# An output tile's matmuls set around another block's mixing products, and ten weight subtractions moved from VectorE to GpSimd

## The chip, the cores and the metric

The kernel runs on one core of a Trainium2 chip. The metric is device time in microseconds (us) of one execution, the median over several. The core has five engines with queues of their own, and each works its queue in order: TensorE (PE, with its weight loads shown as PEld), VectorE (DVE), ScalarE (ACT), GpSimd (POOL) and SyncE (SP), which here only issues DMAs. What one engine owes another is told by semaphores.

## What is computed

Three blocks follow each other on two sequences of 768 tokens with 512 features: local attention with a few global columns, then a mixing layer over tokens and channels, then a second mixing layer with a gate. From the reference, cut to what matters here:

```python
# first mixing layer: U 768x32, V 32x768, w_ch1 512x2048, w_ch2 2048x512
xt = x.transpose(0, 2, 1)
h = xt @ U @ V
u = x + h.transpose(0, 2, 1)
ch = np.maximum(u @ w_ch1, 0.0) @ w_ch2
x = u + ch
# second mixing layer: w_k 512x1024, w_v 1024x512, w_r 512x512
xk = mu_k * x + (1.0 - mu_k) * x_prev
xr = mu_r * x + (1.0 - mu_r) * x_prev
k = np.maximum(xk @ w_k, 0.0)
v = k * k @ w_v
r = 1.0 / (1.0 + np.exp(-(xr @ w_r)))
out = r * v
```

The weights come as 64-bit floats. "Second block" in the title of the change is the second sequence of the batch: its products `h` with U and V.

## The kernel before, in words

**Numbers in two parts.** Every float32 factor of a large product is held as a high part (rounded to TensorE's fp32r format) and a low part (the rest), and each product is three matmuls: high by high, high by low, low by high (`PASS`). A weight goes through one conversion (`conv_steps`, lines 645 to 678): a DMA brings a block of 128x512 64-bit floats into a staging tile `stg` (three of them); DVE cuts the lower word (`cvt`, line 655); ACT scales the upper word (`c1`, line 660, tile `cvc`, four of them); DVE joins them (`c2`, line 664) and sets the sign (`c3`, line 668); ACT rounds the high part (line 672); and the low part is a subtraction, high from value (line 676), on POOL or on DVE. A `cvc` tile is free for the fourth conversion after it only when that subtraction has read it.

**Queue of conversions.** `queue_weight` (lines 697 to 709) appends conversions to a list, and `bg` runs them one at a time between other steps. For the weights of the second mixing layer (`wr` 4 blocks, `wk` 8, `wv` 8) every second subtraction is put on DVE by these two lines, the others stay on POOL; those of w1 and w2 are all on POOL:

```python
707  if name in ("wr", "wk", "wv") and kk % 2:
708      steps[-1] = ("lo", lambda z, f=steps[-1][1]: f(z, "DVE"))
```

**The stages.** The attention comes first, planned by a list scheduler of the kernel's own (`Flow`), with the first sequence's mixing products and the first quarter of w1 laid into it. The rest is written out in order by `weave`, which mixes streams of steps; a scheduler of the framework then orders each engine's queue. The token axis of both sequences together is cut into three chunks `c` of 512, the 2048 hidden features into four groups `g`. For each `g`: `ch1` (matmuls into tiles `aps`, line 926; ACT writes the high part of the result `rs`, line 930, DVE the low part, line 934), then `ch2` (`m_ch2`, lines 942 to 952: four output tiles `o`, each 12 matmuls into a PSUM bank `bps`, over four `f` of `rs`, and a DVE addition into the running sum `yp`, line 952). For `g` from 1 on, chunks 1 and 2 of `ch1` go through seven products of sums and differences (tiles `pps`, line 1019, and DVE additions, line 1023).

**PSUM.** There are eight banks of 128x512: four of kind "a" (`aps`, `kps`, `prs`, some `pps`) and four of kind "t" (`bps`, `hps`, `gps`, the other `pps`). A tile waits until the bank that it takes has been read.

**Around the first place of the change.** After the attention, the second sequence is transposed, multiplied by U (`gps`, line 825), and then by V: eight matmuls `hps` (line 856), four of 256 columns and four of 512, each followed by a DVE addition into `yp` (line 861). They are woven with the four output tiles of `ch2` of `g` 0, chunk 0. Three of those tiles come ahead of the 256-column products, the fourth (`o` 3) behind them:

```python
1181  weave(u1[6:8], c0[:1])
1182  weave(c0[1:3])
1183  for kk in range(4):
1184      u1[8 + kk]()                 # hps of 256 columns, kk
1185      u_split(1, kk, slot_d, 1)    # two parts of the sum: ACT line 899, DVE line 901
1186  weave(c0[3:])                    # output tile o 3
1187  weave(u1[12:])                   # the four hps of 512 columns
```

**Around the second place.** The conversions of `wr` and `wk` run during the last quarter (`g` 3) of `ch1` and `ch2`, those of `wv` at the end of `ch2` and during the gate's products (`prs`, line 1241, whose banks ACT frees with the sigmoid, line 1245). After them come `kps` (line 1221) with its low part `kl` on POOL (line 1231), and `pvs` (line 1256). The same code stands a second time in the program for inputs with wider windows; it is not run here.

Of the kernel before, what the change touches and what calls it, by code (L numbers as in the profile page):

```python
# [13 lines left out]
ALU = mybir.AluOpType  # L14
# [195 lines left out]
def body(tc, out, q, k, v, lim, UV, w1, w2, mu_kr, wk, wv, wr):  # L210
    nc = tc.nc
    with ExitStack() as ctx:
# [8 lines left out]
        yp = const.tile([128, 4, 2 * (S + 1)], F32, name="yp")  # L221
# [394 lines left out]
        def path(general):  # L616
            if general:
                attention_general()
            with ExitStack() as pctx, ExitStack() as fence:
# [6 lines left out]
                def bank(tag, nm):  # L626
                    return pp_.tile([128, 512], F32, tag=tag, name=nm, bufs=banks[tag])
# [69 lines left out]
                def queue_weight(name, src, kt, n, sl):  # L697
                    view = [s.rearrange("p (l k n) -> p l k n", l=2, n=n) for s in sl]
                    per = kt // len(sl)
                    wt[name] = (view, per)  # L700
                    for c0 in range(0, n, 512):
                        for kk in range(kt):
                            hi = view[kk // per][:, 0, kk % per, c0:c0 + 512]
                            lo = view[kk // per][:, 1, kk % per, c0:c0 + 512]
                            s = src[kk * 128:(kk + 1) * 128, c0:c0 + 512]
                            steps = conv_steps((128, 512), hi, lo)
                            if name in ("wr", "wk", "wv") and kk % 2:
                                steps[-1] = ("lo", lambda z, f=steps[-1][1]: f(z, "DVE"))
                            bgq.append((lambda d, s=s: nc.sync.dma_start(out=d, in_=s), steps))

                def wsl(name, l, kk, c0, n):
                    view, per = wt[name]
                    return view[kk // per][:, l, kk % per, c0:c0 + n]
# [32 lines left out]
                def queue_g(g, s1, s2):  # L746
                    if s1:
                        queue_weight(("w1", g), w1[:, g * 512:(g + 1) * 512], 4, 512, [s1("w1s")])
                    if s2:
                        queue_weight(("w2", g), w2[g * 512:(g + 1) * 512, :], 4, 512, [s2("w2s")])  # L750
# [156 lines left out]
                def chunk(buf, kk, c, shift=0):  # L907
                    if c == 0:
                        return [(0, 512, buf[:, kk, 1 - shift:513 - shift])]
                    if c == 2:  # L910
                        return [(0, 512, buf[:, kk, 1026 - shift:1538 - shift])]
                    return [(0, 256, buf[:, kk, 513 - shift:769 - shift]),
                            (256, 512, buf[:, kk, 770 - shift:1026 - shift])]


                PASS = ((0, 0), (0, 1), (1, 0))
                NG = 4
                rs = {}
# [13 lines left out]
                def ch1_low(g, c, f):  # L932
                    r = rs[g, c]
                    nc.vector.scalar_tensor_tensor(out=r[:, 1, f, :], in0=rs[g, c, f], scalar=0.0,  # L934
                                                   in1=r[:, 0, f, :].bitcast(F32), op0=ALU.max, op1=ALU.subtract)

                def m_ch1(g, c, f, mk=None):
                    ch1_mm(g, c, f, mk)
                    ch1_high(g, c, f)
                    ch1_low(g, c, f)  # L940

                def m_ch2(g, c, o):
                    r = rs[g, c]
                    ps = bank("t", "bps")
                    n = 0
                    for f in range(4):
                        for lw, lx in PASS:
                            nc.tensor.matmul(ps, lhsT=wsl(("w2", g), lw, f, o * 128, 128), rhs=r[:, lx, f, :],  # L948
                                             start=(n == 0), stop=(n == 11))
                            n += 1  # L950
                    for a, e, ys in chunk(yp, o, c):
                        nc.vector.tensor_tensor(out=ys, in0=ps[:, a:e], in1=ys, op=ALU.add)  # L952

                diffs, sums = [], {}

# [113 lines left out]
                def weave(*streams):  # L1069
                    items = []  # L1070
                    for n, s in enumerate(streams):
                        items += [((x + 0.5) / len(s), n, x, f) for x, f in enumerate(s)]
                    for *_, f in sorted(items, key=lambda v: v[:3]):
                        f()
# [4 lines left out]
                def st_ch2(g, c):  # L1079
                    return [lambda o=o: m_ch2(g, c, o) for o in range(4)]  # L1080
# [96 lines left out]
                u1, c0 = u_steps(1), st_ch2(0, 0)  # L1177
# [2 lines left out]
                    u_split(1, kk, slot_d, 0)  # L1180
                weave(u1[6:8], c0[:1])
                weave(c0[1:3])
                for kk in range(4):
                    u1[8 + kk]()
                    u_split(1, kk, slot_d, 1)
                weave(c0[3:])
                weave(u1[12:])
                actx.close()
                open_slots("sc")
# [117 lines left out]
                assert not bgq  # L1307

        path(False)
        slow = nc.values_load(flag_i[0:1, 0:1], min_val=0, max_val=1)  # L1310
        with tc.If(slow > 0):
            path(True)
# [22 lines left out]
```

## Time and profile before

| | us |
|---|---|
| three runs | 511.73, 511.78, 514.96 |
| median | 511.78 |
| the profiled execution's own time | 512.37 |
| its span, first to last instruction | 510.6 |
| PE busy, matmuls | 495.5 |
| DVE busy | 351.3 |
| ACT busy | 248.4 |
| POOL busy | 166.8 |

The profiled execution took 1.77 us beyond its span, and lies 0.59 us above the median of the runs. The granted TensorE clock is 0.999 over the span. A matmul of 512 columns is recorded at 390 ns, but matmuls overlap: a run of 48 of them in the chain takes 10.88 us, 0.227 us each.

### The profile page before, as it was taken

The numbers are of one execution on the slowest core, as the hardware profiler recorded it, in microseconds if no ns is written. First come the engines' busy times: TensorE is split into PE (matmuls) and PEld (weight loads), VectorE is DVE, ScalarE is ACT, GpSimd is POOL, SyncE is SP. The second block draws the span as 40 slices with busy tenths as digits, with TensorE's granted clock in tenths as the row PEclk, the third lists the DMA queues.
The fourth block names the chain that finished last, engine by engine and source line by source line (L and its number), as shares of the span: only waits on it lengthen the run. The fifth ranks groups of instructions, "written<-read, shape, count | busy, mean of one in ns | idle before, by whom it ended". The sixth has DMA issues, their size and how long they took to land.

```text
span 510.6 us, 8677 instructions
## 1 busy us (share of the span) xinstructions
PE 495.5 (97%) x3278; PEld 403.5 (79%) x3278; DVE 351.3 (69%) x756; ACT 248.4 (49%) x566; POOL 166.8 (33%) x217
## 2 busy tenths in 40 slices
PE   7899999999999999999999999999999999999995
PEld 4677688778877888888888887888888888888885
DVE  7899988999998879558794599999055057301211
ACT  6999986554432533025330275736883167013400
POOL 7767685020560534005440033122530034002400
PEclk9999999999999999999999999999999999999999
DMA  8888733310334023300242025333001000100011
GB/s 325 295 310 293 238 113 121 122 42 1 124 101 148 0 83 120 127 1 13 81 155 83 0 64 155 113 107 99 0 21 42 21 1 0 56 28 1 0 44 46
DMA packets 13586, 47.18 MB, mean 92 GB/s; under 512 B 1760, under 2 KB 2144, under 8 KB 13536
## 3 DMA queue, kind: packets, MB, share of 16 engines
q1 hardware_dynamic: 13248, 46.28, 27.0%
q8 instruction: 28, 0.46, 0.4%
q10 hardware_dynamic: 288, 0.26, 0.2%
q14 instruction: 22, 0.18, 0.1%
HBM read 43.39 MB, written 3.15 MB: 91 GB/s over the span
## 4 chain that ended last, share of the span: by engine, by line
PE 72%; DVE 20%; DMA 2%; ACT 2%; issue 2%; POOL 1%; ACTq 0%; DVEq 0%; POOLq 0%; SPq 0%
PE bps L948 19%; PE pvs L1256 13%; PE kps L1221 13%; PE pps L1019 9%; PE aps L926 6%; PE prs L1241 6%; DVE cvc L664 3%; DVE P L471 2%; DVE cvc L668 2%; PE tp L498 2%; PE s L463 2%; DMA stg<-in_w_dram 2%; DVE rs L934 1%; DVE sums L972 1%; DVE yp L952 1%
## 5 line engine op out<-in xcount | busy, mean ns | idle before, releaser
L948 PE MATMUL bps<-rs,w2s 128*128 128x512 f32 x576 | 132.4, 390 | 1.2 <-DVE rs L934 0.6
L948 PEld LDWEIGHTS bps<-rs,w2s 128*128 128x128 f32 x576 | 107.8, 188 | 25.2 <-DVE rs L934 1.0
L926 PE MATMUL aps<-us,w1s 128*128 128x512 f32 x288 | 67.9, 391 | 0.0
L1221 PE MATMUL kps<-mix,wk 128*128 128x512 f32 x288 | 65.8, 389 | 0.0
L1231 POOL TENSOR_TENSOR kl<-kf,kh 128x512 fp32r<-128x512 f32 x24 | 31.5, 1313 | 99.5 <-ACT kh L1230 99.5
L1221 PEld LDWEIGHTS kps<-mix,wk 128*128 128x128 f32 x288 | 54.1, 188 | 11.2
L926 PEld LDWEIGHTS aps<-us,w1s 128*128 128x128 f32 x288 | 53.7, 188 | 11.1
L1256 PE MATMUL pvs<-wv,kh 128*128 128x512 f32 (+1 forms) x208 | 60.4, 373 | 0.0
L676 POOL TENSOR_TENSOR w1s<-cvc,w1s 128x512 fp32r<-128x512 f32 x16 | 24.8, 1569 | 89.6 <-DVE sums L1023 52.9
L664 DVE SCALAR_TENSOR_TENSOR cvc<-cvc,cvt 128x512 uint32<-128x512 uint32 (+1 forms) x53 | 51.1, 973 | 1.9 <-ACT cvc L660 0.9
L660 ACT ACTIVATE cvc<-stg 128x512 f32<-128x512 f32 (+1 forms) x53 | 35.1, 674 | 28.9 <-DMA stg<-in_w_dram 13.4
L491 POOL TENSOR_SCALAR P<-P,sm 128x192 f32<-128x192 f32 x96 | 42.1, 462 | 16.3 <-DVE sm L485 6.7
L1256 PEld LDWEIGHTS pvs<-wv,kh 128*128 128x128 f32 x208 | 38.1, 188 | 6.9
L479 ACT ACTIVATE P<-P,nm 128x192 f32<-128x192 f32 x96 | 42.5, 447 | 1.1 <-DVE nm L471 1.0
L1229 DVE SCALAR_TENSOR_TENSOR kf<-kps,kf 128x512 f32<-128x512 f32 x16 | 11.0, 689 | 46.0 <-ACT kf L1225 46.0
L952 DVE TENSOR_TENSOR yp<-bps,yp 128x512 f32<-128x512 f32 (+1 forms) x64 | 33.5, 547 | 8.0 <-PE bps L948 8.0
L1256 PE MATMUL pvs<-wv,kl 128*128 128x512 f32 (+1 forms) x104 | 38.8, 373 | 0.0
L668 DVE SCALAR_TENSOR_TENSOR cvc<-stg,cvc 128x512 uint32<-128x512 uint32 x52 | 37.4, 727 | 0.4
L655 DVE TENSOR_SCALAR cvt<-stg 128x512 uint32<-128x512 uint32 (+1 forms) x53 | 27.3, 519 | 8.8 <-DMA stg<-in_w_dram 7.4
L1023 DVE TENSOR_TENSOR sums<-pps,sums 128x512 f32<-128x512 f32 x30 | 20.6, 689 | 18.4 <-PE pps L1019 17.9
L1241 PE MATMUL prs<-wr,mix 128*128 128x512 f32 x144 | 33.1, 389 | 0.0
L1259 DVE TENSOR_TENSOR sg<-pvs,sg 128x512 f32<-128x512 f32 (+1 forms) x13 | 8.4, 647 | 35.5 <-PE pvs L1256 35.5
(142 smaller groups left out, 796.2 us busy)
## 6 DMA issues: line engine op xcount, KB each, us to landing
stg<-in_w_dram SPq DMA_DIRECT2D x32, 512.0 KB, 4.2
vin<-in_v_dram SPq DMA_DIRECT2D x8, 768.0 KB, 5.8
KK<-in_k_dram SPq DMA_DIRECT2D x7, 768.0 KB, 6.3
stg<-in_wk_dram SPq DMA_DIRECT2D x8, 512.0 KB, 4.0
stg<-in_wv_dram SPq DMA_DIRECT2D x8, 512.0 KB, 3.5
out_dram<-sg SPq DMA_DIRECT2D x11, 256.0 KB, 2.0
QS<-in_q_dram SPq DMA_DIRECT2D x7, 384.0 KB, 6.1
stg<-in_wr_dram SPq DMA_DIRECT2D x4, 512.0 KB, 3.6
```

Of the source, the lines that this page charges most:

```text
L479: nc.scalar.activation(out=Px, in_=Px, func=ACTF.Exp, scale=-1.0, bias=z["nm"][:, i, x:x + 1], accum_out=z["sm"][:, i, x:x + 1])
L491: engine.tensor_scalar(out=Px, in0=Px, scalar1=z["sm"][:, i, x:x + 1], scalar2=1.0, op0=ALU.mult, op1=ALU.mult)
L660: nc.scalar.activation(out=z["c"].bitcast(F32), in_=parts(z)[1].bitcast(F32), func=ACTF.Copy, scale=2.0 ** -112)
L664: nc.vector.scalar_tensor_tensor(out=z["c"], in0=z["c"], scalar=3, in1=z["t"], op0=ALU.logical_shift_left, op1=ALU.bitwise_or)
L668: nc.vector.scalar_tensor_tensor(out=z["c"] if plain is None else plain, in0=parts(z)[1], scalar=0x80000000, in1=z["c"], op0=ALU.bitwise_a ...
L926: nc.tensor.matmul(rs[g, c, f], lhsT=wsl(("w1", g), lw, kk, f * 128, 128), rhs=us[c][:, lx, kk, :], start=(kk == 0 and n == 0), stop=(kk = ...
L948: nc.tensor.matmul(ps, lhsT=wsl(("w2", g), lw, f, o * 128, 128), rhs=r[:, lx, f, :], start=(n == 0), stop=(n == 11))
L952: nc.vector.tensor_tensor(out=ys, in0=ps[:, a:e], in1=ys, op=ALU.add)
L1019: nc.tensor.matmul(t, lhsT=a(lw, k, j), rhs=b(lx, k), start=(not on and k == 0 and m == 0), stop=(k == 1 and m == 2), skip_group_check=n i ...
L1221: nc.tensor.matmul(ps, lhsT=wsl("wk", lw, kk, f * 128, 128), rhs=xk[:, lx, kk, :], start=(n == 0), stop=(n == 11))
L1241: nc.tensor.matmul(pr, lhsT=xr[:, lx, kk, t * 128:(t + 1) * 128], rhs=wsl("wr", lw, kk, 0, 512), start=(n == 0), stop=(n == 11))
L1256: nc.tensor.matmul(pv, lhsT=ks[c][lx][:, f, t * 128:(t + 1) * 128], rhs=wsl("wv", lw, f, c0, c1 - c0), start=(n == 0), stop=(n == 23))
```

## The change

It does two things. First, `m_ch2` is cut into the matmuls (`ch2_mm`, which can do a part of the four `f`) and the addition (`ch2_add`); for output tile `o` 3 of `g` 0, chunk 0, the matmuls of `f` 0 and 1 are put ahead of the second sequence's four products of 256 columns, and those of `f` 2 and 3 with the addition behind them. Second, the two lines that put every second low part of `wr`, `wk` and `wv` on DVE are gone, so that all 20 are on POOL.

```diff
@@ queue_weight
                             steps = conv_steps((128, 512), hi, lo)
-                            if name in ("wr", "wk", "wv") and kk % 2:
-                                steps[-1] = ("lo", lambda z, f=steps[-1][1]: f(z, "DVE"))
                             bgq.append((lambda d, s=s: nc.sync.dma_start(out=d, in_=s), steps))
@@ m_ch2
+                bs = {}
+
+                def ch2_mm(g, c, o, fs=range(4)):
+                    r = rs[g, c]
+                    if 0 in fs:
+                        bs[g, c, o] = bank("t", "bps")
+                    for f in fs:
+                        for n, (lw, lx) in enumerate(PASS):
+                            nc.tensor.matmul(bs[g, c, o], lhsT=wsl(("w2", g), lw, f, o * 128, 128), rhs=r[:, lx, f, :],
+                                             start=(f == 0 and n == 0), stop=(f == 3 and n == 2))
+
+                def ch2_add(g, c, o):
+                    for a, e, ys in chunk(yp, o, c):
+                        nc.vector.tensor_tensor(out=ys, in0=bs[g, c, o][:, a:e], in1=ys, op=ALU.add)
+
                 def m_ch2(g, c, o):
-                    r = rs[g, c]
-                    ps = bank("t", "bps")
-                    n = 0
-                    for f in range(4):
-                        for lw, lx in PASS:
-                            nc.tensor.matmul(ps, lhsT=wsl(("w2", g), lw, f, o * 128, 128), rhs=r[:, lx, f, :],
-                                             start=(n == 0), stop=(n == 11))
-                            n += 1
-                    for a, e, ys in chunk(yp, o, c):
-                        nc.vector.tensor_tensor(out=ys, in0=ps[:, a:e], in1=ys, op=ALU.add)
+                    ch2_mm(g, c, o)
+                    ch2_add(g, c, o)
@@ path
                 weave(c0[1:3])
+                ch2_mm(0, 0, 3, (0, 1))
                 for kk in range(4):
                     u1[8 + kk]()
                     u_split(1, kk, slot_d, 1)
-                weave(c0[3:])
+                ch2_mm(0, 0, 3, (2, 3))
+                ch2_add(0, 0, 3)
                 weave(u1[12:])
```

The scheduler turns this into other queues. On PE, at the second sequence's products, before (`bps` are the output tiles of `ch2`, `hps` the products with V, `aps` the next `ch1`):

```order
L948 MATMUL bps<-rs,w2s 128x512 x36
L856 MATMUL hps<-uv 128x256 x4
L948 MATMUL bps<-rs,w2s 128x512 x12
L856 MATMUL hps<-uv 128x512 x3
L926 MATMUL aps<-us,w1s 128x512 x4
L856 MATMUL hps<-uv 128x512
L926 MATMUL aps<-us,w1s 128x512 x92
```

and now, in the same place:

```order
L948 MATMUL bps<-rs,w2s 128x512 x42
L854 MATMUL hps<-uv 128x256 x3
L948 MATMUL bps<-rs,w2s 128x512 x3
L854 MATMUL hps<-uv 128x256
L948 MATMUL bps<-rs,w2s 128x512 x3
L854 MATMUL hps<-uv 128x512 x2
L924 MATMUL aps<-us,w1s 128x512 x4
L854 MATMUL hps<-uv 128x512
L924 MATMUL aps<-us,w1s 128x512 x2
L854 MATMUL hps<-uv 128x512
L924 MATMUL aps<-us,w1s 128x512 x90
```

Six matmuls of output tile `o` 3 stand ahead of the products, three more ahead of the last of the 256-column ones, three behind it; the last two products of 512 columns went two places further back.

On DVE at the same products, from the addition of output tile `o` 2 on, before (`raw` and `cvc` belong to the conversion of the next weights, `us` is the low part of the sum):

```order
L952 TENSOR_TENSOR yp<-bps,yp 128x512
L861 TENSOR_TENSOR yp<-hps,yp 128x256 x3
L901 TENSOR_TENSOR us<-yp,us 128x256 x3
L861 TENSOR_TENSOR yp<-hps,yp 128x256
L733 TENSOR_TENSOR raw<-cvc,raw 128x256
L664 SCALAR_TENSOR_TENSOR cvc<-cvc,cvt 128x512
L901 TENSOR_TENSOR us<-yp,us 128x256
L952 TENSOR_TENSOR yp<-bps,yp 128x512
L861 TENSOR_TENSOR yp<-hps,yp 128x512 x4
```

and now:

```order
L953 TENSOR_TENSOR yp<-bps,yp 128x512
L731 TENSOR_TENSOR raw<-cvc,raw 128x256
L664 SCALAR_TENSOR_TENSOR cvc<-cvc,cvt 128x512
L859 TENSOR_TENSOR yp<-hps,yp 128x256 x3
L899 TENSOR_TENSOR us<-yp,us 128x256 x3
L859 TENSOR_TENSOR yp<-hps,yp 128x256
L953 TENSOR_TENSOR yp<-bps,yp 128x512
L899 TENSOR_TENSOR us<-yp,us 128x256
L859 TENSOR_TENSOR yp<-hps,yp 128x512 x4
```

The two conversion steps moved ahead of the additions of the products; between the first row and the last the same instructions stand, in another order.

On DVE during the last `ch1` (`g` 3), from the last additions of the sums' products on, before (`wr` and `wk` rows are low parts of weights, `rs<-aps` the low parts of `ch1`'s tiles, `cvc` and `cvt` conversion steps):

```order
L1023 TENSOR_TENSOR sums<-pps,sums 128x512 x2
L676 TENSOR_TENSOR wr<-cvc,wr 128x512
L1027 SCALAR_TENSOR_TENSOR rs<-sums,rs 128x512 x2
L1027 SCALAR_TENSOR_TENSOR rs<-pps,rs 128x512
L1023 TENSOR_TENSOR sums<-pps,sums 128x512
L676 TENSOR_TENSOR wr<-cvc,wr 128x512
L664 SCALAR_TENSOR_TENSOR cvc<-cvc,cvt 128x512
L1027 SCALAR_TENSOR_TENSOR rs<-sums,rs 128x512
L668 SCALAR_TENSOR_TENSOR cvc<-stg,cvc 128x512
L664 SCALAR_TENSOR_TENSOR cvc<-cvc,cvt 128x512
L934 SCALAR_TENSOR_TENSOR rs<-aps,rs 128x512
L668 SCALAR_TENSOR_TENSOR cvc<-stg,cvc 128x512
```

and now:

```order
L1028 TENSOR_TENSOR sums<-pps,sums 128x512 x2
L1032 SCALAR_TENSOR_TENSOR rs<-sums,rs 128x512 x2
L1032 SCALAR_TENSOR_TENSOR rs<-pps,rs 128x512
L1028 TENSOR_TENSOR sums<-pps,sums 128x512
L664 SCALAR_TENSOR_TENSOR cvc<-cvc,cvt 128x512 x2
L1032 SCALAR_TENSOR_TENSOR rs<-sums,rs 128x512
L668 SCALAR_TENSOR_TENSOR cvc<-stg,cvc 128x512 x2
L932 SCALAR_TENSOR_TENSOR rs<-aps,rs 128x512
L655 TENSOR_SCALAR cvt<-stg 128x512
L664 SCALAR_TENSOR_TENSOR cvc<-cvc,cvt 128x512
L932 SCALAR_TENSOR_TENSOR rs<-aps,rs 128x512
L668 SCALAR_TENSOR_TENSOR cvc<-stg,cvc 128x512
```

The low parts are gone from the queue and the conversion steps closed up. Behind the last row shown, up to the fourth `rs<-aps`, stood before: `rs<-aps`, `cvt`, `wk`, `cvc` (664), `cvt`, `cvc` (668), `rs<-aps`, `cvc` (664), `cvt`, `cvc` (668), `cvc` (664), `rs<-aps`; and stand now: `cvt`, `cvc` (664), `cvc` (668), `rs<-aps`, `cvt`, `cvc` (664), `cvt`, `cvc` (668), `rs<-aps`. On POOL's queue the order of the weights is as before, with twice as many rows of each: four `wr`, eight `wk`, eight `wv`, then the 24 `kl`. SP issues the same DMAs in the same order.

## Rows read from the trace of the kernel before

**Rows 1.** The page, busy us, share of the span, instructions:

```profile
PE 495.5 (97%) x3278; PEld 403.5 (79%) x3278; DVE 351.3 (69%) x756; ACT 248.4 (49%) x566; POOL 166.8 (33%) x217
```

**Rows 2.** Who PE waited for: total us, times, longest us:

```profile
PE hps L856 <- DVE yp L952: 1.0, 1, 1.0
...
PE bps L948 <- DVE rs L934: 0.6, 1, 0.6
PE bps L948 <- DVE yp L952: 0.6, 1, 0.6
...
PE pps L1019 <- DVE sums L1023: 0.3, 1, 0.3
```

**Rows 3.** Stretches: length; PE, PEld, DVE, ACT, POOL busy; clock, DMA share, GB/s:

```profile
105.00:150.00 45.00, 44.44 (x197) 36.45 (x196) 44.73 (x73) 21.49 (x39) 18.81 (x12) 1.00 0.19 60
295.60:310.00 14.40, 14.40 (x64) 11.60 (x62) 14.40 (x25) 10.53 (x19) 5.66 (x4) 1.00 0.32 102
```

**Rows 4.** Timeline of PE: start, duration (us), instruction, [idle before, releaser]:

```profile
103.53 0.38 PE L856 MATMUL hps<-uv 96*128 96x256 f32 x1 [1.03 <-DVE yp L952]
...
146.47 3.89 PE L948 MATMUL bps<-rs,w2s 128*128 128x512 f32 x16 [0.56 <-DVE yp L952]
...
163.31 1.66 PE L1019 MATMUL pps<-diff,w1s 128*128 128x512 f32 x6 [0.25 <-DVE sums L1023]
...
307.66 2.43 PE L948 MATMUL bps<-rs,w2s 128*128 128x512 f32 x10
310.70 30.67 PE L948 MATMUL bps<-rs,w2s 128*128 128x512 f32 x134 [0.61 <-DVE rs L934]
```

**Rows 5.** Timeline of DVE around the second sequence's products and the first sums:

```profile
102.79 0.68 DVE L952 TENSOR_TENSOR yp<-bps,yp 128x512 f32<-128x512 f32 x1
...
107.60 2.47 DVE L861 TENSOR_TENSOR yp<-hps,yp 128x512 f32<-128x512 f32 x4
...
145.58 0.74 DVE L952 TENSOR_TENSOR yp<-bps,yp 128x256 f32<-128x256 f32 x2
...
160.25 3.00 DVE L1023 TENSOR_TENSOR sums<-pps,sums 128x512 f32<-128x512 f32 x4
```

**Rows 6.** Timeline of DVE during the last `ch1` and the weights' conversions:

```profile
295.58 1.27 DVE L676 TENSOR_TENSOR wr<-cvc,wr 128x512 fp32r<-128x512 f32 x1
...
297.97 0.68 DVE L1027 SCALAR_TENSOR_TENSOR rs<-pps,rs 128x512 fp32r<-128x512 f32 x1
...
302.18 0.67 DVE L934 SCALAR_TENSOR_TENSOR rs<-aps,rs 128x512 fp32r<-128x512 f32 x1
302.78 1.45 DVE L668 SCALAR_TENSOR_TENSOR cvc<-stg,cvc 128x512 uint32<-128x512 uint32 x1
...
304.75 0.41 DVE L655 TENSOR_SCALAR cvt<-stg 128x512 uint32<-128x512 uint32 x1
305.08 0.68 DVE L676 TENSOR_TENSOR wk<-cvc,wk 128x512 fp32r<-128x512 f32 x1
...
310.57 1.16 DVE L676 TENSOR_TENSOR wk<-cvc,wk 128x512 fp32r<-128x512 f32 x1
...
354.23 1.59 DVE L664 SCALAR_TENSOR_TENSOR cvc<-cvc,cvt 128x512 uint32<-128x512 uint32 x1
```

**Rows 7.** Timeline of POOL, low parts of the second mixing layer's weights:

```profile
295.00 1.30 POOL L676 TENSOR_TENSOR wr<-cvc,wr 128x512 fp32r<-128x512 f32 x1 [32.45 <-DVE sums L1023]
297.51 1.71 POOL L676 TENSOR_TENSOR wr<-cvc,wr 128x512 fp32r<-128x512 f32 x1 [1.21 <-ACT wr L672]
302.39 1.29 POOL L676 TENSOR_TENSOR wk<-cvc,wk 128x512 fp32r<-128x512 f32 x1 [3.17 <-ACT wk L672]
...
353.93 1.35 POOL L676 TENSOR_TENSOR wv<-cvc,wv 128x512 fp32r<-128x512 f32 x1 [2.54 <-ACT wv L672]
```

**Rows 8.** Timeline of ACT, the first sigmoid:

```profile
348.57 0.60 ACT L1245 ACTIVATE sg<-prs 128x512 f32<-128x512 f32 x1
```

**Rows 9.** The chain that ended last, start, us: the first chunk's `kps`:

```profile
352.25 21.76 PE kps L1221 x96
```

## The prediction

> **What bounds the kernel now.** I read the page's busy times first: PE is busy 495.5 us of the span and DVE 351.3 [rows 1], so whatever does not show up as a gap of PE costs nothing. The second view is the list of what PE waited for [rows 2], the third its timeline with the gaps [rows 4]. Behind the attention PE has four gaps of a quarter us or more, every one ended by DVE: 1.03 us at 103.5 (the fourth 256-column product needs the bank of output tile `o` 2), 0.56 at 146.5 (an output tile needs a bank that DVE reads late), 0.25 at 163.3 (DVE's additions of the sums) and 0.61 at 310.7 (the low part of `rs`). Together they are 2.45 us, half a per cent: the change can win no more than that unless it makes PE's own work shorter, and it has the same matmuls. The fourth view is the busy time by stretch [rows 3]: DVE works 44.73 us of 45 between 105 and 150 and 14.40 of 14.40 between 295.6 and 310. In both places DVE is full and PE runs just behind it, so a delay of DVE there becomes a gap of PE nearly one for one. The last views are the timelines of DVE and POOL in these stretches [rows 5 to 7].
>
> **Part one, the output tile around the products.** It removes, adds and moves no work: the same 12 matmuls, eight products and additions stand in both queues. Six matmuls of 0.227 us (48 take 10.88) now fill 1.36 us ahead of the products, so PE has something to do while DVE reads `o` 2 (from 102.79 [rows 5]), and the gap of 1.03 us goes. The tile takes the bank of `gps`, which DVE has read before 102.79, so it brings no wait of its own; the fourth product stands three matmuls later and may wait a few tenths for its bank.
>
> What is late next is DVE. Its queue is full there and has the same instructions up to the four additions of the 512-column products, which begin at 107.60 [rows 5] in either order: 0.33 + 0.60 us of conversion were pulled ahead of the products' additions and are missing behind them. PE arrives a us earlier at the bank of 146.5, which DVE frees with the additions at 145.58, and at the sums of 163.3, which DVE makes from 160.25 to 163.25 [rows 4, 5]. There DVE is ahead only by what the order dropped on the way (one cutting step of 0.33 us in front of 145.58) and by where POOL's subtractions fall between. So the 1.03 us come back in part as longer gaps at these two places. The bounds: all three gaps go, -1.84 us; nothing is left, or the shuffled order of DVE and POOL costs a little, +0.6. I take -0.9, half of the three.
>
> **Part two, ten subtractions from DVE to POOL.** Each costs DVE 0.60 us from its start to the next one's start where nothing disturbs (302.18 to 302.78 [rows 6]) and POOL 1.29 to 1.30 (1.71 and more where it waits) [rows 7]. POOL is busy 5.66 us of 14.40 in the critical stretch [rows 3] and has the time. But the two engines get in each other's way. While POOL's subtraction runs from 302.39 to 303.68, DVE's step `c3`, begun at 302.78, takes 1.45 us where its like take 0.68: it ends 0.55 us behind POOL's, as if it had begun only then [rows 6, 7]. The subtraction of 295.58 takes 1.27 beside POOL's of 295.00, the step of 354.23 takes 1.59 beside that of 353.93. An operation that reads PSUM is not held: the one of 297.97 takes 0.68 while POOL is busy from 297.51 to 299.22. Over the ten subtractions that POOL does between 295.00 and 353.93 (first and last in [rows 7]) the operation of DVE that was held lost 0.59, 0, 0.77, 0.48, 0.38, 0.51, 0.71, 0.91, 1.11 and 0.91 us, the mean is 0.64. The mechanism: DVE loses, for each subtraction moved, about what it saves, when the operation behind it reads SBUF.
>
> The page "SBUF — State Buffer" of the Trainium skill, section "SBUF: two separate sides", speaks against this part: the port pair that GpSimd shares with VectorE is a lock held for a whole instruction, and a VectorE operation with two SBUF inputs then blocks fully. The trace agrees (the held step ends 0.55 us behind POOL's). By the rule alone, with POOL always first, every subtraction would cost DVE 1.29 us, the price of the second rival below; the rows give less because POOL often comes in while DVE reads PSUM.
>
> Now the sum up to the fourth `rs<-aps`, on which PE waits at 310.7. Before: from 295.58, 21 operations of 0.60 and three cuts of 0.33 make 13.6 us; measured are 14.99 to 310.57, the 1.4 more being the 0.59 and 0.77 above. After: 19 operations and four cuts, 11.4 + 1.34 = 12.74 us (three low parts gone, one `c3` and one cut drawn in front by the closing up). Held time: behind the first `wr`, seven subtractions of POOL fall into this stretch (`wr` three, `wk` four) where before there were three. At 0.64 each they cost 4.5 us and the fourth `rs` is done 2.2 us later than before; at 1.29 it is 9.0, 6.8 later; with none held it is 2.25 earlier, and PE's gap of 0.61 goes. The new order has, behind each operation that reads PSUM, a conversion step that reads SBUF, and each cut stands directly ahead of the step that needs it, a hole in which POOL gets in: these are the cases of 302.78 (0.77) and 354.23 (0.91) [rows 6], and the second is the row nearest to most of the seven. I take 0.9: 6.3 us, the fourth `rs` done at 295.58 + 12.74 + 6.3 = 314.6 in place of 310.57, so PE's gap grows by 4.05 us. PE is otherwise not touched in between: it waits in its own queue for the `rs` parts in order, and the additions of `yp` behind them have their four banks. Bounds: -0.6 and +6.8.
>
> **The tail of part two.** The eight subtractions of `wv` are now all on POOL. They have until 374 (where the chain goes on to `pvs` at 352.25 + 21.76 [rows 9]) and cost nothing there. But ACT's conversion steps stand between the sigmoids that free the banks of `prs` for `kps`: the first sigmoid ends at 348.57 + 0.60 = 349.17 [rows 8], 3.1 us ahead of the first `kps` at 352.25 [rows 9]. In the new order two more conversions stand ahead of it. At 0.60 + 0.60 + 0.33 of DVE and 0.9 held each they are 4.9 us, 1.8 over that cover; with the DVE low parts gone ahead of it nothing is left. Bounds 0 and +1.8; I take +0.7, since the low parts no longer done cover rather more than half.
>
> The DMAs are the same and in the same order; each goes out when a staging tile has been read, so they follow DVE. POOL's `kl` come behind `wv` and have 2.7 us (12 matmuls) each at 1.3.
>
> **Sum.** -0.9 + 4.05 + 0.7 = +3.85 us. The profiled execution took 512.37, so 516.2 by it; it lies 0.59 above the median of the runs (511.78), and a median is what is asked: 515.6 us, 0.75% slower. A measurement of this kernel can tell about 1% from no change, 5.1 us, so this is within it.
>
> **Rivals.** One: POOL is free and the split keeps its gain. POOL idles two thirds of the time [rows 1], and DVE gives up ten operations in stretches where it is full; if POOL's subtractions fall beside PSUM reads (as that of 297.51) DVE gets ahead, all four gaps go, and 511.78 - 2.45 = 509.3 us. Against it: of ten, nine held DVE. Chance 0.13.
>
> Two, the other side: DVE is held for the whole of nearly every subtraction. Place: from 295.6 to the fourth `rs`; price 7 x 1.29 = 9.0 us less the 2.25 saved, +6.8; with 1.8 at the sigmoids and -0.9 from part one it is +7.7, 519.5 us. For it: 0.91 and 1.11 occur, and DVE, waiting in order for ACT's step that waits for a `cvc` tile that POOL has not yet read, opens more holes for POOL. Against: the mean is 0.64. It decides (over 1%) from 1.08 us per subtraction, where -0.9 + 7x - 2.25 + 0.7 passes 5.1. Chance 0.22.
>
> Three: part one does not do what it says, because the fourth product's wait is only moved, and part two costs as forecast: 515.6 + 0.9 = 516.5. Chance 0.05.
>
> **How the numbers follow.** The forecast gets 0.60: held time between 0.64 and 1.08 each, 513 to 516.9. The range of eight in ten: from 511.5 (part one at full gain, 0.64 or a little less held) to 518.8 (short of rival two's end), so that half of rival one and a third of rival two stay out. Slower by over 1% (from 516.9): rival two's 0.22 and 0.06 from the upper edge of the forecast, 0.28. Faster by over 1% would need 5.1 us where the gaps are 2.45: 0.01. Within 1%: 0.71.
>
> **What would show it.** Right: the wait of `hps` for `yp` gone from PE's list or down to tenths; a wait of `pps` for the sums near 1 us; the wait of `bps` for `rs` grown from 0.6 to 4 or 5 us, in two or three pieces; DVE's conversion steps `c2` and `c3` between 295 and 315 often 1.2 to 1.9 us long beside POOL's subtractions. Wrong: `c2` and `c3` there at 0.68 as before, or PE without a gap at its first `bps` of `g` 3; a gap at a place not named; a wait of `pvs` for POOL.

## The result and the profile after

The changed kernel takes 518.82 us (median of four runs, 517.73 to 519.63) beside 512.08 for the kernel before in the same comparison: a ratio of 1.0118 with a 95% interval of 1.0076 to 1.0159, 3.9 to 8.1 us slower. The forecast was 3.85 us slower, 515.6; the measured time stands at the very end of the range (518.8). By its median the change is slower by more than 1% (the interval begins at 0.76%), a case that had a chance of 0.28.

The busy times of the page of the kernel after answer to [rows 1], and the list of what PE waited for to [rows 2]:

```profile
PE 499.1 (96%) x3278; PEld 405.6 (78%) x3278; DVE 353.7 (68%) x746; ACT 248.9 (48%) x566; POOL 179.1 (35%) x227
```

```profile
PE bps L948 <- DVE rs L932: 4.3, 2, 2.5
...
PE pps L1024 <- DVE sums L1028: 1.0, 1, 1.0
...
PE bps L948 <- ACT rs L928: 0.5, 1, 0.5
...
PE hps L854 <- DVE yp L859: 0.2, 1, 0.2
```

Three of the four gaps of [rows 4] changed as the edit suggests: that of `hps` went from 1.0 to 0.2, that of `bps` for `yp` is gone, that for the sums grew from 0.3 to 1.0. The fourth, PE waiting for `rs`, grew from 0.6 to 4.8 (4.3 for DVE's parts and 0.5 for ACT's). But PE is also busy 3.6 us longer (499.1 against 495.5) with the same 3278 matmuls, and waits alone do not explain that. The stretches of the kernel after say why; the clock is the third number from the end of each row:

```profile
295.00:310.00 15.00, 14.52 (x65) 11.65 (x63) 14.43 (x19) 9.72 (x19) 9.89 (x7) 1.00 0.23 74
310.00:320.00 10.00, 5.71 (x14) 3.96 (x14) 9.89 (x13) 4.92 (x9) 4.89 (x4) 0.69 0.55 170
320.00:333.00 13.00, 13.00 (x57) 10.68 (x56) 12.90 (x19) 8.25 (x15) 3.56 (x3) 0.97 0.33 109
```

Between 310 and 320 PE's clock was 0.69 on the mean, where the kernel before has 1.00:

```profile
310.00:320.00 10.00, 9.39 (x42) 7.72 (x42) 9.35 (x16) 4.91 (x9) 2.53 (x2) 1.00 0.58 165
```

By single microseconds of the trace after:

```profile
313.00:314.00 1.00, 0.13 (x1) 0.00 (x0) 1.00 (x2) 0.12 (x1) 0.49 (x1) 0.93 0.96 344
314.00:315.00 1.00, 0.00 (x0) 0.00 (x0) 1.00 (x4) 0.00 (x0) 0.00 (x0) 0.50 0.22 86
...
320.00:321.00 1.00, 1.00 (x4) 0.79 (x3) 1.00 (x2) 0.14 (x1) 0.55 (x1) 0.66 0.82 328
321.00:322.00 1.00, 1.00 (x6) 0.78 (x6) 1.00 (x2) 0.00 (x0) 0.00 (x0) 1.00 0.05 21
```

The granted clock falls from full to half (2.4 to 1.2 GHz) while PE stands still in its third wait, and comes back at about 320.7, after PE has worked for five us. The timeline of PE shows both prices, waits and slow work:

```profile
307.80 1.52 PE L948 MATMUL bps<-rs,w2s 128*128 128x512 f32 x6
309.80 0.49 PE L948 MATMUL bps<-rs,w2s 128*128 128x512 f32 x1 [0.48 <-ACT rs L928]
312.07 1.05 PE L948 MATMUL bps<-rs,w2s 128*128 128x512 f32 x3 [1.78 <-DVE rs L932]
315.64 33.04 PE L948 MATMUL bps<-rs,w2s 128*128 128x512 f32 x134 [2.51 <-DVE rs L932]
348.51 11.04 PE L1248 MATMUL prs<-wr,mix 128*128 128x512 f32 x48
```

The kernel before has, for the same end of the stage:

```profile
341.20 11.04 PE L1241 MATMUL prs<-wr,mix 128*128 128x512 f32 x48
```

From the first `bps` of `g` 3 to the first `prs` it took 341.20 - 307.66 = 33.54 us before and 348.51 - 307.80 = 40.71 after, 7.17 more. Waits: 0.48 + 1.78 + 2.51 = 4.77 against 0.61, +4.16. The 134 matmuls behind the last wait: 33.04 against 30.67 [rows 4], +2.37, that is the clock. The ten in front, cut into pieces: 1.52 + 0.49 + 1.05 = 3.06 against 2.43, +0.63: a single matmul takes 0.49 here, where in a run each adds 0.23. The sum is 7.16. The 0.63 is no price of its own: in both kernels the 134 begin 0.13 us after DVE goes on behind the fourth `rs` (310.57 and 310.70 before, 315.51 and 315.64 after), so what the pieces took longer only shortened the waits. By cause, the fourth `rs` came 4.80 us later (with 0.14 taken off, by which the trace after runs later there), and the clock cost 2.37.

One execution starts later than another by up to a us and a half, in the attention's loads. So the traces are compared from the first matmul `bps` behind the attention on, at 93.65 us before and 94.24 after: to the span's end 416.95 and 423.46 us, 6.5 more. The stage above gives 7.17 of it; ahead of the stage 0.45 is gained, and behind it 0.2.

Now DVE in that stretch, with [rows 6] beside it:

```profile
296.09 2.60 DVE L1032 SCALAR_TENSOR_TENSOR rs<-sums,rs 128x512 fp32r<-128x512 f32 x2 [0.29 <-ACT rs L1031]
298.61 0.68 DVE L1032 SCALAR_TENSOR_TENSOR rs<-pps,rs 128x512 fp32r<-128x512 f32 x1
...
299.81 2.38 DVE L664 SCALAR_TENSOR_TENSOR cvc<-cvc,cvt 128x512 uint32<-128x512 uint32 x2
...
304.52 1.19 DVE L655 TENSOR_SCALAR cvt<-stg 128x512 uint32<-128x512 uint32 x1
305.81 1.59 DVE L664 SCALAR_TENSOR_TENSOR cvc<-cvc,cvt 128x512 uint32<-128x512 uint32 x1
...
309.77 1.65 DVE L668 SCALAR_TENSOR_TENSOR cvc<-stg,cvc 128x512 uint32<-128x512 uint32 x1
...
312.46 1.59 DVE L664 SCALAR_TENSOR_TENSOR cvc<-cvc,cvt 128x512 uint32<-128x512 uint32 x1
...
314.91 0.68 DVE L932 SCALAR_TENSOR_TENSOR rs<-aps,rs 128x512 fp32r<-128x512 f32 x1
```

and POOL, with [rows 7] beside it:

```profile
295.14 6.50 POOL L676 TENSOR_TENSOR wr<-cvc,wr 128x512 fp32r<-128x512 f32 x4 [32.45 <-DVE sums L1028]
304.12 2.72 POOL L676 TENSOR_TENSOR wk<-cvc,wk 128x512 fp32r<-128x512 f32 x2 [2.49 <-ACT wk L672]
309.33 1.54 POOL L676 TENSOR_TENSOR wk<-cvc,wk 128x512 fp32r<-128x512 f32 x1 [2.48 <-ACT wk L672]
312.15 1.35 POOL L676 TENSOR_TENSOR wk<-cvc,wk 128x512 fp32r<-128x512 f32 x1 [1.28 <-ACT wk L672]
```

Each long step of DVE lies on one of POOL's, and ends soon behind it: 305.81 + 1.59 = 307.40 beside 306.84, 312.46 + 1.59 = 314.05 beside 313.50. The same steps take 0.68 alone (two together 1.28, a cut 0.41). What they lost: 1.32 + 1.10 + 0.78 + 0.91 + 0.97 + 0.91 = 5.99 us over eight subtractions, 0.75 each. The step that reads PSUM at 298.61 lies inside POOL's four and takes 0.68.

### The profile page after: what moved, and what is told of

Read it like the earlier page. It is cut to its first block, busy times and chain, and to the rows that moved or that the text cites. A ratio compares the mean times of both kernels' runs of the same rounds, so it can differ in the third digit from the quotient of the medians.

```text
span 517.7 us, 8687 instructions
## 1 busy us (share of the span) xinstructions
PE 499.1 (96%) x3278; PEld 405.6 (78%) x3278; DVE 353.7 (68%) x746; ACT 248.9 (48%) x566; POOL 179.1 (35%) x227
## 4 chain that ended last, share of the span: by engine, by line
PE 72%; DVE 19%; DMA 3%; issue 2%; ACT 1%; POOL 1%; DVEq 0%; POOLq 0%; SPq 0%; ACTq 0%
PE bps L948 19%; PE pvs L1263 13%; PE kps L1228 13%; PE pps L1024 8%; PE aps L924 6%; PE prs L1248 6%; DMA stg<-in_w_dram 3%; DVE P L471 3%; DVE cvc L664 3%; DVE cvc L668 2%; PE tp L498 2%; PE s L463 2%; DVE cvt L655 1%; DVE rs L932 1%; DVE sums L977 1%
## 5 line engine op out<-in xcount | busy, mean ns | idle before, releaser
L948 PE MATMUL bps<-rs,w2s 128*128 128x512 f32 x576 | 135.5, 395 | 4.9 <-DVE rs L932 4.3
L948 PEld LDWEIGHTS bps<-rs,w2s 128*128 128x128 f32 x576 | 109.4, 191 | 30.1 <-DVE rs L932 4.9
L668 DVE SCALAR_TENSOR_TENSOR cvc<-stg,cvc 128x512 uint32<-128x512 uint32 x52 | 44.5, 866 | 0.4
L655 DVE TENSOR_SCALAR cvt<-stg 128x512 uint32<-128x512 uint32 (+1 forms) x53 | 30.8, 584 | 8.1 <-DMA stg<-in_w_dram 7.6
L1212 DVE SCALAR_TENSOR_TENSOR mixf<-yp,mu,mixt 128x512 f32<-128x512 f32 (+1 forms) x32 | 19.3, 632 | 22.0 <-ACT mixt L1211 22.0
```

Of the source, the lines that this page charges most:

```text
L655: nc.vector.tensor_scalar(out=z["t"], in0=parts(z)[0], scalar1=2.0 ** -29, scalar2=7.0, op0=ALU.mult, op1=ALU.min)
L668: nc.vector.scalar_tensor_tensor(out=z["c"] if plain is None else plain, in0=parts(z)[1], scalar=0x80000000, in1=z["c"], op0=ALU.bitwise_a ...
L948: nc.tensor.matmul(bs[g, c, o], lhsT=wsl(("w2", g), lw, f, o * 128, 128), rhs=r[:, lx, f, :], start=(f == 0 and n == 0), stop=(f == 3 and ...
```

## The experiments

Edits are shown against the changed kernel where nothing else is said, and "..." marks what is cut. Times of the kernel before in these comparisons are 512.50 (first four runs), 512.18 (next four) and 512.37 us (last two).

**Part one alone.** The two lines of `queue_weight` are back.

```diff
                             steps = conv_steps((128, 512), hi, lo)
+                            if name in ("wr", "wk", "wv") and kk % 2:
+                                steps[-1] = ("lo", lambda z, f=steps[-1][1]: f(z, "DVE"))
```

> Part one alone, the low parts as before. Theory (the split frees about 0.6 us, the rest of the cost is part two's): PE's wait of hps falls from 1.03 us to 0.2, the wait of 0.56 at 146.5 goes, the wait of pps grows from 0.25 to 1.05; the wait of bps for rs stays at 0.6 and the granted clock at 1.0 from 310 to 320; 511.5 us. Rival (DVE, full, gives the whole gain back): 512.1 us. Rival (the split itself makes the later waits longer): 513 us or more, with a wait of bps for rs well over 0.6 us.

512.34 us, ratio 0.9994 (0.9983 to 1.0004): between 0.9 us faster and 0.2 slower. The waits of `hps`, `yp` and the sums came as expected (none over 0.2, none, 0.9), but PE waited 1.70 us for `rs`, not 0.6, with a clock of 1.00 throughout. DVE's queue is that of the kernel before in that stretch. The difference is one meeting of DVE and POOL, in the trace of part one alone:

```profile
307.30 0.67 DVE L664 SCALAR_TENSOR_TENSOR cvc<-cvc,cvt 128x512 uint32<-128x512 uint32 x1
307.90 1.51 DVE L655 TENSOR_SCALAR cvt<-stg 128x512 uint32<-128x512 uint32 x1
```

```profile
307.51 1.62 POOL L676 TENSOR_TENSOR wk<-cvc,wk 128x512 fp32r<-128x512 f32 x1 [4.36 <-ACT wk L672]
```

and in that of the kernel before, at the same instructions:

```profile
307.83 0.67 DVE L664 SCALAR_TENSOR_TENSOR cvc<-cvc,cvt 128x512 uint32<-128x512 uint32 x1
308.43 0.41 DVE L655 TENSOR_SCALAR cvt<-stg 128x512 uint32<-128x512 uint32 x1
```

```profile
308.04 3.14 POOL L676 TENSOR_TENSOR wk<-cvc,wk 128x512 fp32r<-128x512 f32 x1 [4.36 <-ACT wk L672]
```

Both times POOL's subtraction is recorded from 0.21 us behind the start of DVE's step on, and lasts beyond its end. Then in the one POOL went on first, and DVE's cut took 1.51; in the other DVE's cut and the steps behind it did, and POOL's subtraction took 3.14. Which of the two comes first decides over 1.1 us of PE, though the order of both queues is the same. Each was seen in one trace; how often either happens was not measured.

**Part two alone.** The low parts all on POOL; the output tile in one piece, as before. Against the kernel before this is the whole edit:

```diff
-                            if name in ("wr", "wk", "wv") and kk % 2:
-                                steps[-1] = ("lo", lambda z, f=steps[-1][1]: f(z, "DVE"))
```

> Part two alone, the output tile in one piece as before. Theory (held conversion steps make the last rs late by 4 us, and PE, having idled, then runs some 6 us at half clock): waits of bps for rs of 4 to 5 us in two or three pieces, granted clock 0.5 for about 6.7 us behind them, 512.1 + 4.2 + 3.4 = 519.6 us. Rival (the two parts work on each other, the clock falls only where both are there): 516.3 us with a clock of 1.0. Rival (part two costs nothing alone): 512.1 us.

519.11 us, ratio 1.0130 (1.0114 to 1.0147). PE waited 0.47, 1.77 and 2.18 us for `rs`, and the 134 matmuls took 32.37 us. The clock fell here at about 312.3, when PE had just gone on behind the second wait (0.66 between 312 and 313, 0.50 from there to 319), and was full again from 319.2 on:

```profile
315.55 32.37 PE L946 MATMUL bps<-rs,w2s 128*128 128x512 f32 x134 [2.18 <-DVE rs L932]
```

The whole cost is part two's; the parts do not need each other for it.

**Of part two only the low parts of `wv`.** The split stays.

```diff
+                            if name in ("wr", "wk") and kk % 2:
+                                steps[-1] = ("lo", lambda z, f=steps[-1][1]: f(z, "DVE"))
```

> The change, but with every second low part of wr and wk on DVE as before: of part two only the four low parts of wv go to POOL. Theory (the cost lies with wr and wk in the stretch up to the fourth rs; wv has time): waits as in part one alone, clock 1.0, 511.5 us. Rival (the cost goes by the number of subtractions on POOL, wherever they are): four of ten moved, 511.5 + 0.4 x 7.3 = 514.4 us. Rival (the first kps is late): a wait of kps of up to 1.8 us, 513.3 us.

511.76 us, ratio 0.9986 (0.9975 to 0.9998); the wait for `rs` is 0.63, no `kps` waits, and the clock is 1.00. POOL takes four more subtractions here and nothing is lost: it matters where they are done, not how many.

**POOL's subtraction cut short.** For `wr` and `wk` it covers 64 of 512 columns; the products with `wr` and `wk` read the high part in place of the low one, so the low parts of these two weights are left out.

```diff
+                            if name in ("wr", "wk"):
+                                steps[-1] = ("lo", lambda z, hi=hi, lo=lo: nc.gpsimd.tensor_tensor(
+                                    out=lo[:, :64], in0=z["c"].bitcast(F32)[:, :64], in1=hi.bitcast(F32)[:, :64], op=ALU.subtract))
...
+                    l = 0 if name in ("wr", "wk") else l
```

> The change, but POOL's subtraction for wr and wk covers 64 of 512 columns, and the products of wr and wk read the high part where they read the low one (the low parts of these two weights are left out); the queues have the same instructions in the same order. Theory (DVE is held as long as POOL's subtraction runs): the conversion steps of DVE between 295 and 315 take 0.68 us nearly all, the waits of bps for rs fall to 0.6 or less, clock 1.0, 518.8 - 4.2 - 3.4 - 0.6 = about 510.6 us. Rival (the order of DVE's queue, with conversion steps ahead of the rs parts, makes the rs late): waits of 4 to 5 us and half clock as in the changed kernel, 518.8 us. Rival (transfers of the weights are late): waits of DVE for stg in their place, 514 us or more.

511.96 us, ratio 0.9987 (0.9975 to 0.9999). The order of DVE's queue, of ACT's and of POOL's is that of the changed kernel to the last instruction, yet DVE's steps take their own time, POOL's are short, and PE waits 0.50 us with the clock at 1.00. From the end of the sums DVE needs 14.87 us to the end of the fourth `rs`, 19.79 in the changed kernel. Short subtractions also free the `cvc` tiles sooner, but that is not where the time went: DVE's waits between its steps are longer here (2.1 us against 1.1), and what is gone is the held time. DVE, POOL and PE of this kernel:

```profile
299.12 1.29 DVE L664 SCALAR_TENSOR_TENSOR cvc<-cvc,cvt 128x512 uint32<-128x512 uint32 x2
...
310.41 0.68 DVE L936 SCALAR_TENSOR_TENSOR rs<-aps,rs 128x512 fp32r<-128x512 f32 x1
```

```profile
298.07 0.32 POOL L708 TENSOR_TENSOR wr<-cvc,wr 128x64 fp32r<-128x64 f32 x1 [1.72 <-ACT wr L672]
```

```profile
311.15 11.22 PE L952 MATMUL bps<-rs,w2s 128*128 128x512 f32 x48 [0.50 <-DVE rs L936]
```

The rival that blamed the order of DVE's queue falls: with the same order and short subtractions the fourth `rs` is in time. (Of the 1.4 us by which the time misses the expected 510.6, some 0.9 lie ahead of the mark: the first `bps` comes at 95.09 in this trace and at 94.24 in that of the changed kernel. From there to the end are 415.7 us, 7.8 less than in the changed kernel and 1.25 less than before.)

**PE kept busy in its waits.** Ten matmuls, whose product the next output tile overwrites, are put ahead of the two that wait longest.

```diff
-                    if 0 in fs:
+                    if 0 in fs and (g, c, o) != (3, 0, 1):
                         bs[g, c, o] = bank("t", "bps")
+                    if (g, c, o) == (3, 0, 0):
+                        bs[3, 0, 1] = bank("t", "fill")
                     for f in fs:
                         for n, (lw, lx) in enumerate(PASS):
+                            if (g, c, o) == (3, 0, 0):
+                                for _ in range({(2, 1): 4, (3, 1): 6}.get((f, n), 0)):
+                                    nc.tensor.matmul(bs[3, 0, 1], lhsT=wsl(("w2", g), 0, 0, 0, 128), rhs=r[:, 0, 0, :],
+                                                     start=True, stop=True)
```

> The change, with ten idle-filling matmuls on PE (their product is overwritten by the next output tile's first matmul): four ahead of the matmul that waits 1.78 us and six ahead of the one that waits 2.51 us. DVE and POOL have the same steps up to there. Theory (3.4 us of the change's cost come from PE running at half clock after it has idled): the three waits of bps shrink to about 0.5, 0.9 and 1.2 us, the last rs comes when it came, the granted clock stays at 1.0 from 310 to 322, and about 515.3 us, or up to 2 us more if the ten matmuls, which the scheduler also counts, bring a wait further on, which would have its own row. Rival (the clock falls for another reason, such as PE's mean load over a longer time or what other engines do): clock 0.5 there again and 518.8 us.

518.40 us, ratio 1.0116 (1.0092 to 1.0139). The clock stayed at 1.00 in every microsecond from 308 to 323, but the time hardly moved (0.4 us, within the noise of both). Its PE timeline shows the shrunk waits and two new ones:

```profile
311.12 1.04 PE L954 MATMUL bps<-rs,w2s 128*128 128x512 f32 x3 [0.87 <-DVE rs L932]
312.00 1.55 PE L952 MATMUL fill<-rs,w2s 128*128 128x512 f32 x6
314.70 0.73 PE L954 MATMUL bps<-rs,w2s 128*128 128x512 f32 x2 [1.15 <-DVE rs L932]
...
343.38 3.00 PE L954 MATMUL bps<-rs,w2s 128*128 128x512 f32 x12 [0.67 <-DVE yp L959]
...
358.55 21.83 PE L1234 MATMUL kps<-mix,wk 128*128 128x512 f32 x95 [1.30 <-ACT sg L1258]
```

So the idling did bring the clock down, and work in the gaps kept it up. But of the 2.4 us won, 0.67 + 1.30 us come back as waits further on. PE arrives earlier at work that DVE and ACT have not got ready; DVE has no idle time left there (busy 19.00 us of 19 between 333 and 352, 18.64 in the changed kernel). The ten matmuls also made the scheduler order the later conversion steps otherwise, so which share of these two waits the changed kernel would have at full clock is not separated. Its own rows bound it: its first sigmoid ends at 357.79, and its `kps` begins at 359.39; without the 2.37 of the clock PE would stand there at 357.02 and wait 0.8.

```profile
357.19 0.60 ACT L1252 ACTIVATE sg<-prs 128x512 f32<-128x512 f32 x1
```

**All low parts on DVE**, none on POOL, with the split.

```diff
+                            if name in ("wr", "wk", "wv"):
+                                steps[-1] = ("lo", lambda z, f=steps[-1][1]: f(z, "DVE"))
```

> The split of part one, and all 20 low parts of wr, wk and wv on DVE, none on POOL. Theory (what a subtraction on POOL costs DVE by holding it is about what doing it costs DVE): from the end of the sums, 295.4, DVE has 20 steps of 0.60 and two cuts of 0.33 up to the fourth rs, none held: 308.1, before PE needs it at 309.9; so the wait of bps for rs goes, and the time is 0.6 below the split with the low parts as before, about 511.2 us beside a kernel before of 512.5. Rival (DVE is the bound there and each further low part on it costs PE 0.60): four more in the stretch, a wait of 3 us or more, half clock behind it, 517 us or more.

511.56 us, ratio 0.9987 (0.9976 to 0.9998). PE has no wait for `rs` at all: six low parts stand in DVE's queue between the sums and the fourth `rs`, where the changed kernel has none, and DVE is done in time, since none of its steps is held. The rival, that each low part on DVE costs PE its 0.60 us, falls.

**`wr` and `wk` on DVE, `wv` on POOL**, with the split, and once more beside the same without it.

```diff
+                            if name in ("wr", "wk"):
+                                steps[-1] = ("lo", lambda z, f=steps[-1][1]: f(z, "DVE"))
```

> The split of part one, the 12 low parts of wr and wk on DVE and the 8 of wv on POOL: each where the runs so far say that it costs nothing. Theory: no wait of bps for rs, no wait of kps, 511.2 us or a little less, beside a kernel before of 512.5. Rival (the low parts of wk late on DVE delay the sigmoids' banks): a wait of kps or prs of 0.5 to 2 us, 512 to 513.5 us.

511.00 us, ratio 0.9970 (0.9958 to 0.9982). All 144 matmuls of the last `ch2` run without a gap:

```profile
307.31 32.80 PE L950 MATMUL bps<-rs,w2s 128*128 128x512 f32 x144
```

**A stall of middle size:** the split, `wr` on POOL, `wk` and `wv` as before.

```diff
+                            if name in ("wk", "wv") and kk % 2:
+                                steps[-1] = ("lo", lambda z, f=steps[-1][1]: f(z, "DVE"))
```

> The split of part one, of part two only the low parts of wr (four on POOL), wk and wv as before: a stall of middle size. Up to the fourth rs DVE has 20 steps of 0.60 and three cuts of 0.33, 13.0 us, and POOL five or six subtractions; at 0.88 each held, 4.4 to 5.3: the fourth rs is done near 313.3 and PE waits 3 to 4 us in all. Theory (the clock's price comes whole once the waits are long enough together): half clock for some 6 us behind it, 512 + 3 + 3.4 = 518 us. Rival (no fall of the clock at this length): 515 us. Rival (only wk's subtractions matter): 512 us.

516.70 us, ratio 1.0090 (1.0066 to 1.0114). PE waited 0.17 + 1.78 + 0.69 = 2.64 us, less than the 3 to 4 expected, and the clock was at half for 3.4 us, not six. (This is the fastest of the four executions, 515.47 us; the others took 516.23 to 517.38, and what waits and clock cost in them was not traced.) Timeline of PE, and two single microseconds:

```profile
311.37 0.49 PE L950 MATMUL bps<-rs,w2s 128*128 128x512 f32 x1 [1.78 <-ACT rs L930]
312.56 32.21 PE L950 MATMUL bps<-rs,w2s 128*128 128x512 f32 x134 [0.69 <-DVE rs L934]
```

```profile
313.00:314.00 1.00, 1.00 (x3) 0.72 (x3) 0.90 (x3) 0.82 (x2) 0.16 (x1) 0.50 0.08 33
...
316.00:317.00 1.00, 1.00 (x6) 0.81 (x5) 0.94 (x2) 0.70 (x2) 0.00 (x0) 1.00 0.30 82
```

The 134 matmuls took 32.21, 1.54 more than at full clock. So the clock's price is no fixed sum: 1.54, 1.70 and 2.37 us on these 134 matmuls in three kernels, and none in part one alone, whose one wait of 1.70 us stood behind an unbroken run.

**Without the split, and with it once more.** `wr` and `wk` on DVE and `wv` on POOL, in the kernel before:

```diff
-                            if name in ("wr", "wk", "wv") and kk % 2:
+                            if name in ("wr", "wk"):
```

> The kernel before with one line of another kind: the low parts of wr and wk on DVE, those of wv on POOL, the output tile in one piece. Theory (the split is worth the three waits that it trades, 1.84 us for about 1.1 to 1.2; the weights' part is worth the wait of 0.6): PE waits of 1.0 for hps, 0.6 for yp, 0.3 for the sums and none for rs; 511.6 us beside a kernel before of 512.2, and 0.6 above the version with the split. Rival (the split is worth nothing): 511.0 us, as with the split. Rival (the split is what makes the difference): 512.2 us, as before.

> The split with wr and wk on DVE and wv on POOL once more, beside the same version without the split on the same chip. Theory: 0.6 us below it, 0.3% below the kernel before. Rival (its first result was chance): level with it.

511.03 us, ratio 0.9966 (0.9955 to 0.9978) without the split, 511.13 us, ratio 0.9973 (0.9963 to 0.9983) with it. In the traces the split has less to wait for (0.88 + 0.56 + 0.41 without, 0.18 + 0.95 with it; from the first `bps` to the end 415.8 and 415.5 us); in the times nothing is left of it. The best version of the study is thus a change of one line to the kernel before: 0.3% faster than it.

## Why the prediction was right or wrong

**What bounds the kernel: right.** PE is the bound, DVE stands just behind it between 295 and 310, and a delay of DVE there becomes a gap of PE.

**Part one: right in kind, somewhat too large.** Said were -0.9 us of three waits of 1.84; the waits after are 0.18 + 1.05 = 1.23, 0.6 less, and by the times of part one alone the gain is 0.3 with an interval that holds zero. "What is late next is DVE", at the sums, held: 1.05, where "near 1" was forecast. What the argument left out is why DVE does not follow at once. In front of the sums stands a cut that waits for a weight's transfer, 0.19 us before and 0.76 after:

```profile
159.91 0.43 DVE L655 TENSOR_SCALAR cvt<-stg 128x512 uint32<-128x512 uint32 x1 [0.19 <-DMA stg<-in_w_dram]
```

```profile
160.05 0.43 DVE L655 TENSOR_SCALAR cvt<-stg 128x512 uint32<-128x512 uint32 x1 [0.76 <-DMA stg<-in_w_dram]
160.39 3.00 DVE L1028 TENSOR_TENSOR sums<-pps,sums 128x512 f32<-128x512 f32 x4
```

**Part two, the held steps: right in kind and nearly in size.** The fourth `rs` was forecast at 314.6 and was done at 315.51, in a trace that runs 0.14 later there: 4.80 us later than before, where 4.05 was said. That PE's gap grew by 4.16, so near to 4.05, is luck: 0.63 of the delay went into the pieces of PE's ten matmuls, of which the forecast knew nothing. The sum's parts: 12.74 us of work and 6.3 held were said; measured are 19.79 us from the end of the sums (295.72), so 7.05 above the work, 5.99 of it in held steps and 1.06 in short waits of DVE between steps, which the sum put at nothing. The held time came out near because two errors cancel: eight of POOL's subtractions fell in, the first `wr` among them, not seven, and each held DVE for 0.75 where 0.9 was taken. The short-subtraction run shows that this holding is the cause, and the version with all low parts on DVE that the work itself fits.

**The step that failed is "PE's gap grows by 4.05 us" as the whole price of the stage.** To the forecast, a late `rs` cost its own delay and nothing behind it. The stage took 7.17 us more: 4.80 for the delay, 0.75 above the forecast, and 2.37 of half clock behind the wait, for which the sum had no term. These 3.1 us are most of the distance between 515.6 and 518.8. (The terms of part one and of the tail came out 0.45 us better than said, 0.45 and 0.2 gained in the traces against -0.9 and +0.7; and the kernel before took 0.3 us more in this comparison than the 511.78 from which the forecast started.) That the range still reaches the measured time, to its last tenth, is luck: its upper end was drawn from longer holds, not from the clock. In the kernel before the clock falls only behind the last matmul, so the price could not be read there; that a stall of several us might bring it should have stood in the range as a cost of its own.

**The tail at the sigmoids: hidden.** +0.7 us was said, and no `kps` waited. The cover shrank as argued: by PE's timeline `kps` began 2.9 us behind the end of the first sigmoid before (352.08; the forecast's 3.1 is from the chain), and 359.39 - 357.79 = 1.6 after. Without the 2.37 us of half clock it would have been used up. The two terms, the clock and the tail, lie over each other: PE made slow is also PE that waits less. The run that kept the clock up agrees, with a `kps` that waits 1.30 and a time 0.4 lower, not 2.4; how much of that is due to its other order of conversion steps stays open.

**The second rival named nearly the right time by the wrong way.** It gave 519.5 with a hold of 1.29 us per subtraction. The hold was 0.75, and the rest came from the clock. The first rival (POOL free, four gaps gone) falls with the waits of 4.77 us.

## What to carry to other kernels

A low part moved from VectorE to GpSimd is not free because GpSimd is idle: in the stretch where VectorE is full, GpSimd's step of 1.3 us held VectorE for 0.75 us on the mean and saved it 0.60. So keep such work off GpSimd where TensorE waits for VectorE next, and give it to GpSimd where TensorE does not: the low parts of `wv` cost nothing there, though VectorE was busy 10.39 of 11 us between 341 and 352 in that run. Price a stall of TensorE by its length and by what the clock does behind it, and look then at whether the engines behind it would have been ready any sooner.

## What was not expected of the hardware

**The cut is held too.** `cvt` reads one SBUF operand, and the forecast counted operations with two. It took 1.19, 1.50 and 1.51 us beside POOL's subtractions in the changed kernel, 0.41 alone. The Trainium skill, "SBUF — State Buffer", section "Who interferes with whom", says that a single-input step contends only in a mode that takes both port pairs, which a tensor_scalar can enter; this agrees with a step that takes 0.33 us from start to start where two-input steps of the same size take 0.60. No run here changes its mode.

**Holding goes either way.** The pair of traces above shows both: 1.51 us of DVE's cut in the one, 3.14 of POOL's subtraction in the other. The Trainium skill, "SBUF — State Buffer", section "Who interferes with whom", says that the order of issue decides who blocks. The pair does not show that: in both, POOL's subtraction is recorded 0.39 us ahead of the cut, and once the cut went first.

**The clock fell behind waits of less than 2.6 us each.** In the changed kernel PE had done ten matmuls in three pieces, with waits of 0.48, 1.78 and 2.51 us behind them, and the granted clock went to half in the last wait. With `wr` alone on POOL the waits behind such pieces were 0.17, 1.78 and 0.69, and it fell in the last again. In part two alone it fell behind waits of 0.47 and 1.77, ahead of the third. One wait of 1.70 between long runs, and waits of 0.49, 0.87 and 1.15 with ten matmuls more in them, left it at full. What decides between them was not measured further.
